# Four attention heads between the halves of two rank mixes, in an attention kernel with two mixer layers

## The chip, the cores and the metric

One core of a Trainium2 chip runs the whole program. The metric is the device time of one execution in microseconds (us), taken as the median of several runs. Three runs of the kernel before gave 1568.89, 1569.15 and 1572.46 us.

## What is computed

Four batches (448 tokens, 12 heads of 64 channels) go through three layers. The reference, cut to what matters:

```python
q_n, k_n = rmsnorm(q, g_q), rmsnorm(k, g_k)
scores = (q_n @ k_n.transpose(0, 1, 3, 2)) / sqrt(64)
x = softmax(scores) @ v                       # then heads side by side: (4, 448, 768)

u = x + ((x.transpose(0, 2, 1) @ U) @ V).transpose(0, 2, 1)      # "rank mix", rank 32
x = u + relu(u @ w_ch1) @ w_ch2                                  # 768 -> 3072 -> 768

u = x + (relu(x.transpose(0, 2, 1) @ w_tok1) @ w_tok2).transpose(0, 2, 1)   # "token mix"
out = u + relu(u @ w_ch1b) @ w_ch2b                              # 768 -> 1536 -> 768
```

## The kernel before, in words

Products are made with operands split into a high and a low part (`hi`, `lo` in fp32r), so that one product takes two or three matmuls. The engines' work is issued by a Python program whose blocks are generators. A scheduler then sets the order on each engine's queue. Each queue runs in that order.

**Attention.** `attention` is one generator over 48 heads: 24 of batches b0 and b1, then 24 of b2 and b3. One step of it (`next`) issues the softmax of one head and, in lockstep, the weighing of the head before. Softmax takes four chunks of scores: the matmuls into `sc` in PSUM, a maximum `nm` on DVE (L327), an exponential `p` on ACT (L329), a scaling of `p` on POOL (L336). Weighing takes four transposes `pt` (L355), the split into `ph` on ACT (L363) and `pl` on DVE (L367), and eight matmuls into `pv`; `tmp` (L375) and a sum on DVE (L376) end a head. For every second head a pair is loaded and normalised (POOL: `sq`, `qn`, `kn`, L255 and L273; DVE: `ms`, L256) and turned: transposes `tt` on PE (L290), `hi` and `lo` (L298 to L303), then twelve copies on the DMA queue of SP (L312, L313). Outputs of the last 24 heads go through the tile `xo` to memory.

**The first stage** takes the steps of the first 24 heads, with 3 `sc` and 4 `pt` buffers. Then pools are closed and others opened: PSUM has 2 buffers `p` (shared by `pt` and the transposes `pt_x` of a mix), 1 buffer `v` for `pv`, 2 buffers `s` (`sc` and `ps_u`), 1 buffer `t` (`tt` and `ps_h`) and 2 buffers `m` (the channel mixing).

**The rank mixes.** For each of b0 and b1, `rank_mix` runs two halves of 384 channels. A half has four token chunks `pt_x` (PE), each split on ACT (L428) and DVE (L429), eight matmuls into `ps_h`, a split of that on ACT (L451) and DVE (L452), and three times two matmuls into `ps_u`, whose result is added on DVE (L433), copied on ACT (L434) and subtracted on POOL (L435) by `split_u`.

**Channel mixing.** `ffn("a", ...)` runs 12 groups of two weight chunks. A group has 72 matmuls into `ps_g` and 72 into `ps_x`, for both batches. Each weight chunk comes as 64-bit words by DMA and is prepared on ACT (L125, L130, L144), DVE (L126, L127, L131) and POOL (L134, L145). `run(main, side, ratio)` takes attention steps of the remaining 24 heads between pieces of the channel mixing, in proportion to a weight that each piece yields:

```python
left += t * ratio
while left > 0:
    if next(side, None) is None:
        break
    left -= 1
```

With ratio 24 / 326 * 1.08 the steps are spread over the first eleven groups of the program; the scheduler takes them earlier where PE would be free.

Of the kernel before, what the change touches and what calls it, by code (L numbers as in the profile page):

```python
# [24 lines left out]
def attention_then_two_mixers(  # L25
# [49 lines left out]
    def f(x):  # L75
        return x.bitcast(F32)

    def mm(o, l, r, start, stop):
        nc.tensor.matmul(o, lhsT=l, rhs=r, start=start, stop=stop)  # L79
# [28 lines left out]
    def psum(kind, shape, name):  # L108
        pool = pools[kind]
        return pool.tile(shape, F32, tag=pool.name, name=name)  # L110
# [87 lines left out]
    def w1_chunk(nm, w, j):  # L198
        if f"{nm}1_{j}" in cache:
            return again(f"{nm}1_{j}")  # L200
        return load_w(w[:, j * P:(j + 1) * P].rearrange("(cc p) f -> p cc f", p=P), P, DM,
                      keep=f"{nm}1_{j}")
# [215 lines left out]
    def to_tokens(xT, hf):  # L418
        for c in range(NC4):
            pt = psum("p", [CP, HALF], "pt_x")  # L420
            for i in range(3):
                nc.tensor.transpose(
                    pt[:, i * P:(i + 1) * P],
                    xT[:, 3 * hf + i, c * CP:(c + 1) * CP], ident,
                )
            s = pools["new_xs"]()[:CP, :, :HALF]
            hi, lo = s[:, 0], s[:, 1]
            nc.scalar.activation(hi, pt, AF.Copy)  # L428
            nc.vector.tensor_sub(lo, pt, f(hi))  # L429
            yield hi, lo  # L430

    def split_u(xT, cc, pu, u):
        nc.vector.tensor_add(xT[:, cc], pu, xT[:, cc])  # L433
        nc.scalar.activation(u[0][:, cc], xT[:, cc], AF.Copy)  # L434
        pools["split_u"].tensor_sub(u[1][:, cc], xT[:, cc], f(u[0][:, cc]))  # L435

    def new_u():
        return [act.tile([P, CC, S], F32R, tag=t, name="u") for t in ("uh", "ul")]

    def rank_mix(xT, uv):  # L440

        u4, vh, vl = uv
        u = new_u()
        for hf in range(2):
            ph = psum("t", [P, HALF], "ps_h")
            for c, xs in enumerate(to_tokens(xT, hf)):
                for i in range(2):
                    mm(ph, u4[:, c].rearrange("p t r -> p (t r)"), xs[i],
                       c == 0 and i == 0, c == NC4 - 1 and i == 1)
            hst = pools["new_xs"]()[:, 0, :HALF]  # L450
            nc.scalar.activation(hst, ph, AF.Copy)  # L451
            nc.vector.tensor_sub(hst[2 * R:], ph[2 * R:], f(hst[2 * R:]))  # L452
            for i in range(3):
                pu = psum("s", [P, S], "ps_u")
                hs = hst[:, i * P:(i + 1) * P]
                mm(pu, hs, vh, True, False)
                mm(pu, hs, vl, False, True)
                split_u(xT, 3 * hf + i, pu, u)
        return u

    def token_mix(xT, w):

# [31 lines left out]
    def ffn(nm, w1, w2, xs, us, after, early=None, half=None, last=lambda: None,  # L494
            mid=lambda i: None):

        n = w1.shape[1] // P  # L500

        def first(u, ws):
            pg = psum("m", [P, S], "ps_g")
            wh, wl = ws
            for cc in range(CC):
                fs = slice(cc * P, (cc + 1) * P)
                mm(pg, wh[:, fs], u[0][:, cc], cc == 0, False)
                mm(pg, wl[:, fs], u[0][:, cc], False, False)
                mm(pg, wh[:, fs], u[1][:, cc], False, cc == CC - 1)
            s = pools["g"].tile([P, 2, S], F32R, tag="g", name="gs")  # L510
            gh, gl = s[:, 0], s[:, 1]
            nc.scalar.activation(gh, pg, AF.Relu)
            nc.vector.scalar_tensor_tensor(  # L513
                gl, pg, 0.0, f(gh), op0=ALU.max, op1=ALU.subtract
            )
            return gh, gl

        def second(xT, gs, ws, done=None):
            for dc in range(CC):
                px = psum("m", [P, S], "ps_x")  # L520
                ds = slice(dc * P, (dc + 1) * P)
                for i, ((gh, gl), (wh, wl)) in enumerate(zip(gs, ws)):
                    mm(px, wh[:, ds], gh, i == 0, False)
                    mm(px, wl[:, ds], gh, False, False)
                    mm(px, wh[:, ds], gl, False, i == len(gs) - 1)
                nc.vector.tensor_add(xT[:, dc], px, xT[:, dc])  # L526
                if done and dc % 3 == 2:
                    done(dc // 3)

        for j0 in range(0, n, G):  # L530
            js = range(j0, j0 + G)
            w1s = early if early and not j0 else [w1_chunk(nm, w1, j) for j in js]
            if 0 < j0 < n - G:
                gs = [[] for _ in xs]
                for ws in w1s:
                    for i, u in enumerate(us):
                        gs[i].append(first(u, ws))
                        yield 3.4
                w2s = [w2_chunk(nm, w2, j) for j in js]
                for i, xT in enumerate(xs):  # L540
                    second(xT, gs[i], w2s)
                    yield 3.4 * G
            else:
                w2s = [w2_chunk(nm, w2, j) for j in js]
                if j0:
                    last()
                for i in range(len(xs)):
                    gs = [first(us[i], ws) for ws in w1s]
                    if j0:
                        mid(i)  # L550
                    yield 3.4 * G
                    second(xs[i], gs, w2s, half and j0 and (lambda h: half(i, h)))
                    yield 3.4 * G
                    if j0:
                        after(i)
# [163 lines left out]
    def run(main, side, ratio):  # L719

        left = 0.0
        for t in main:
# [5 lines that stand above are left out]
        for _ in side:  # L728
            pass

    b0, b1, b2, b3 = range(B)
    xs = [new_x() for _ in range(2)]
    us = [None] * 2
# [5 lines left out]
    with ExitStack() as stack:  # L739
        open_pools(stack, (("hs", 1, 0), ("at", 2, 0)))  # L740
        inner = stack.enter_context(ExitStack())
        AT.update(p=12, ph=4, pl=4)
        open_pools(inner, (("pp", 1, 0), ("s", 3, 1), ("t", 1, 1), ("p", 4, 1)))
        pools["v"] = pools["p"]

        def new_xo():
            return pools["at"].tile([P, S], F32, tag="xo", bufs=1, name="xo")

        att = attention(
            [(b, hp, (), lambda xT=xT, hp=hp: xT[:, hp], lambda dst: None)  # L750
             for b, xT in zip((b0, b1), xs) for hp in range(NP)]
            + [(b, hp, (), new_xo,
                lambda dst, b=b, hp=hp: nc.sync.dma_start(xd[b][hp], dst))
               for b in (b2, b3) for hp in range(NP)], 2 * H)

        for t in att:
            if t == 8:
                pools["late"] = True
                uv = load_uv(False)
                pools["late"] = False  # L760
            if t == 2 * H - 1:
                break
        pools["late"] = True
        w1s = [w1_chunk("a", wa1, j) for j in range(G)]
        pools["late"] = False
        inner.close()
        AT.update(p=8, ph=3, pl=3)
        open_pools(stack, (("pp", 1, 0), ("g", 2 * G + 1, 0), ("p", 2, 1), ("v", 1, 1),
                           ("s", 2, 1), ("t", 1, 1), ("m", 2, 1)))
        pools["new_xs"] = lambda: pools["g"].tile([P, 2, S], F32R, tag="g", name="xs")  # L770
        for i in range(2):
            us[i] = rank_mix(xs[i], uv)


        def mix(i):
            us[i] = token_mix(xs[i], wt)

        def swap():
            for _ in att:
                pass  # L780
            stack.close()
            open_pools(rest, (("wt", 1, 0), ("x3", 1, 0), ("g", 3 * G, 0),
                              ("m", 3, 1), ("s", 2, 1), ("t", 1, 1), ("p", 2, 1)))
            open_pools(first_pair, (("xs", 6, 0), ("uv", 1, 0)))
            pools["new_xs"] = lambda: pools["xs"].tile([P, 2, HALF], F32R, tag="xs", name="xs")
            wt.extend(load_wt())
            kept.extend(load_uv(True))

        run(ffn("a", wa1, wa2, xs, us, mix, w1s, last=swap), att, 24 / 326 * 1.08)

    def fetch(pool, b):
        xT = pool.tile([P, CC, S], F32, tag="xT", name="xT")
# [61 lines left out]
```

## Time and profile before

| what | value |
|---|---|
| median of three runs | 1569.15 us |
| span of the profiled execution, first to last instruction | 1565.9 us |
| median of the runs less that span | 3.25 us |
| PE busy | 1467.3 us (94%) |
| DVE busy | 1124.4 us (72%) |
| POOL busy | 824.9 us (53%) |
| ACT busy | 731.0 us (47%) |
| mean granted clock of TensorE | 0.979 of full speed |

For the profiled execution the span is the time that is known; what lies around it is taken as the 3.25 us by which the median of the runs exceeds it. Shares are of the span. A busy PE counts from a matmul's start to its modelled end, and neighbours overlap, so the spacing of starts is the better measure of what PE can do.

### The profile page before, as it was taken

To read this page: it belongs to the slowest core of one execution; us is meant where nothing else is said; L and a number is where in the kernel's file an instruction comes from. 1 tells how busy PE (TensorE), PEld (TensorE's weight loads), DVE (VectorE), ACT (ScalarE), POOL (GpSimd) and SP (SyncE) were. 2 spreads that over 40 slices of the span, in tenths; PEclk is the share of its full clock that TensorE was granted. 3 is DMA by queue.
4 is the path that set the end of the run, shared out by engine and by line. 5 is a ranking of instruction groups with operands and counts; after the bars stand their busy time and mean duration, and the time that the engine had idled before them with its cause. 6 is when DMAs were issued, how large, how long until landed. Compare 5 with 4: busy or idle time off the path is not lost.

```text
span 1565.9 us, 21838 instructions
## 1 busy us (share of the span) xinstructions
PE 1467.3 (94%) x7522; PEld 1297.9 (83%) x7522; DVE 1124.4 (72%) x1824; ACT 731.0 (47%) x1449; POOL 824.9 (53%) x844
## 2 busy tenths in 40 slices
PE   5888877999999999999999999899999999999998
PEld 3566756888888889888888998789998999988997
DVE  6787977878888887766958776586756764576653
ACT  5786855666666665443624443342322222342311
POOL 6788886987877655554735543042443523103320
PEclk9898969999999999999999999999999999999999
DMA  6456663565654444542515540511212111101202
GB/s 168 118 143 151 153 198 99 168 190 180 196 161 147 142 146 137 183 172 69 184 39 187 187 143 23 163 58 51 71 51 69 43 51 61 66 21 51 71 21 91
DMA packets 103950, 180.97 MB, mean 116 GB/s; under 512 B 10464, under 2 KB 79552, under 8 KB 103840
## 3 DMA queue, kind: packets, MB, share of 16 engines
q1 hardware_dynamic: 103520, 179.58, 37.2%
q8 instruction: 60, 0.98, 0.3%
q14 instruction: 50, 0.41, 0.1%
q10 hardware_dynamic: 320, 0.00, 0.0%
HBM read 107.19 MB, written 36.57 MB: 92 GB/s over the span
## 4 chain that ended last, share of the span: by engine, by line
PE 65%; DVE 15%; DMA 6%; POOL 5%; ACT 4%; issue 4%; SPq 1%; DVEq 0%; POOLq 0%; ACTq 0%
PE ps_x L79 26%; PE ps_g L79 16%; PE ps_p L79 11%; PE sc L79 3%; PE pv L79 2%; PE pt L355 2%; DVE w_bits L126 2%; PE ps_u L79 2%; DVE w_bits L131 2%; PE ps_t L79 2%; DMA qr<-in_q_dram 1%; POOL w_bits L134 1%; DVE w_bits L127 1%; DVE nm L327 1%; POOL w L145 1%
## 5 line engine op out<-in xcount | busy, mean ns | idle before, releaser
L79 PE MATMUL ps_x<-gs,w 128*128 128x448 f32 x2592 | 576.4, 369 | 14.1 <-DVE xT L656 4.2
L79 PEld LDWEIGHTS ps_x<-gs,w 128*128 128x128 f32 x2592 | 484.0, 189 | 62.0 <-DVE xT L526 8.4
L79 PE MATMUL ps_g<-u,w 128*128 128x448 f32 x1584 | 343.7, 369 | 2.0 <-DVE gs L513 1.5
L79 PEld LDWEIGHTS ps_g<-u,w 128*128 128x128 f32 x1584 | 295.3, 188 | 27.8 <-DVE gs L513 1.9
L145 POOL TENSOR_TENSOR w<-w 128x768 fp32r<-128x768 f32 x44 | 85.0, 1941 | 220.0 <-ACT w L144 153.3
L134 POOL TENSOR_TENSOR w_bits<-w_bits,w_round 128x768 uint32<-128x768 uint32 (+3 forms) x80 | 142.1, 1776 | 93.8 <-DVE w_bits L131 34.0
L145 POOL TENSOR_TENSOR w<-w_bits,w 128x768 fp32r<-128x768 f32 (+3 forms) x82 | 147.8, 1809 | 79.8 <-ACT w L144 76.7
L656 DVE TENSOR_TENSOR xT<-ps_x,xT 128x448 f32<-128x448 f32 x216 | 127.9, 617 | 65.4 <-PE ps_x L79 63.6
L526 DVE TENSOR_TENSOR xT<-ps_x,xT 128x448 f32<-128x448 f32 x216 | 131.9, 616 | 39.5 <-PE ps_x L79 36.8
L336 POOL TENSOR_SCALAR p<-p,sm 112x448 f32<-112x448 f32 x192 | 135.4, 718 | 24.7 <-DVE sm L333 20.9
L329 ACT ACTIVATE p<-sc,nm 112x448 f32<-112x448 f32 x192 | 121.7, 635 | 43.6 <-DVE nm L327 37.3
L145 POOL TENSOR_TENSOR w_a<-w_a 128x384 fp32r<-128x384 f32 (+1 forms) x28 | 41.7, 1490 | 186.0 <-DVE w_t L223 142.9
L367 DVE TENSOR_TENSOR pl<-pt,ph 112x448 fp32r<-112x448 f32 x192 | 116.6, 614 | 16.9 <-ACT ph L363 16.4
L327 DVE TENSOR_REDUCE nm<-sc 112x1 f32<-112x448 f32 x192 | 116.1, 613 | 14.7 <-PE sc L79 14.2
L355 PE MATMUL pt<-ident,p 112*112 112x112 f32 x768 | 116.8, 263 | 3.8 <-POOL p L336 3.4
L363 ACT ACTIVATE ph<-pt 112x448 fp32r<-112x448 f32 x192 | 101.4, 544 | 39.9 <-PE pt L355 38.8
L126 DVE TENSOR_SCALAR w_bits<-w_bits 128x768 f32<-128x768 f32 (+3 forms) x80 | 81.9, 1023 | 47.8 <-ACT w_bits L125 47.4
L355 PEld LDWEIGHTS pt<-ident,p 112*112 112x112 f32 x768 | 92.0, 136 | 24.7 <-POOL p L336 6.7
L627 DVE TENSOR_TENSOR pu<-ps_p,pu 128x448 f32<-128x448 f32 x98 | 59.2, 619 | 70.8 <-PE ps_p L79 70.7
L130 ACT ACTIVATE w_round<-w_raw 128x768 uint32<-128x768 uint32 (+3 forms) x80 | 69.8, 872 | 73.9 <-POOL w_bits L134 71.9
L79 PE MATMUL sc<-ks,qs 128*112 128x448 f32 x192 | 81.5, 436 | 21.5 <-ACT p L329 13.3
L144 ACT ACTIVATE w<-w_bits 128x768 fp32r<-128x768 f32 (+3 forms) x82 | 65.6, 818 | 54.5 <-POOL w_bits L134 32.3
(104 smaller groups left out, 2390.6 us busy)
## 6 DMA issues: line engine op xcount, KB each, us to landing
w_raw<-in_moe_w_ch_dram SPq DMA_DIRECT2D x72, 768.0 KB, 4.4
c_a<-w_bits SPq DMA_DIRECT2D x48, 384.0 KB, 3.1
ks<-hi SPq DMA_DIRECT2D x96, 112.0 KB, 2.3
kt<-lo SPq DMA_DIRECT2D x96, 112.0 KB, 2.3
w<-c_a SPq DMA_DIRECT2D x28, 384.0 KB, 3.7
c_b<-w_bits SPq DMA_DIRECT2D x24, 384.0 KB, 3.1
w_a<-c_a SPq DMA_DIRECT2D x20, 384.0 KB, 2.9
w<-c_b SPq DMA_DIRECT2D x16, 384.0 KB, 3.5
```

Of the source, the lines that this page charges most:

```text
L79: nc.tensor.matmul(o, lhsT=l, rhs=r, start=start, stop=stop)
L126: nc.vector.tensor_scalar_max(f(w), f(w), TINY)
L134: nc.gpsimd.tensor_tensor(w, w, r, op=ALU.add)
L145: nc.gpsimd.tensor_sub(lo, w, f(hi))
L327: nc.vector.tensor_reduce(nm, sc, axis=AX.X, op=ALU.max, negate=True)
L329: nc.scalar.activation(p, sc, AF.Exp, bias=nm, accum_out=sm[:, c % 2:c % 2 + 1])
L336: nc.gpsimd.tensor_scalar(x, x, sm[:, i:i + 1], 1.0, op0=ALU.mult, op1=ALU.mult)
L355: nc.tensor.transpose(pt[:, c * CP:(c + 1) * CP], pr[c][:, kc * CP:(kc + 1) * CP], ident[:CP, :CP],)
L363: nc.scalar.activation(ph, pt, AF.Copy)
L367: nc.vector.tensor_sub(pl, pt, f(ph))
L526: nc.vector.tensor_add(xT[:, dc], px, xT[:, dc])
L656: nc.vector.tensor_add(xT[:, dc], px, xT[:, dc])
```

## The change

`rank_mix` becomes a generator, `rank_steps`, that stops after each half; the two first rank mixes run through it, and after each of their four halves one step of `attention` is issued. These are the steps of heads 24 to 27, the first four of b2. The ratio of `run` is cut from 24 to 20 parts accordingly. The other users of `rank_mix` (b2 and b3, later) are as before.

```diff
     def rank_mix(xT, uv):
+        u = new_u()
+        for _ in rank_steps(xT, uv, u):
+            pass
+        return u
+
+    def rank_steps(xT, uv, u):
 
         u4, vh, vl = uv
-        u = new_u()
         for hf in range(2):
...
                 split_u(xT, 3 * hf + i, pu, u)
-        return u
+            yield
...
         for i in range(2):
-            us[i] = rank_mix(xs[i], uv)
-
+            us[i] = new_u()
+            for _ in rank_steps(xs[i], uv, us[i]):
+                next(att)
...
-        run(ffn("a", wa1, wa2, xs, us, mix, w1s, last=swap), att, 24 / 326 * 1.08)
+        run(ffn("a", wa1, wa2, xs, us, mix, w1s, last=swap), att, 20 / 326 * 1.08)
```

The queues are the same up to the first half of the first rank mix. On PE, right after that half's transposes, the order changes so (`ps_h`, `ps_u`: rank mix; `ps_g`: channel mixing of the first group; `sc`: scores of head 24):

```order
 L79 MATMUL ps_h<-xs,w 128x384
 L422 MATMUL pt_x<-ident,xT 112x128 x3
+L79 MATMUL ps_h<-xs,w 128x384 x4
+L79 MATMUL ps_u<-w,xs 128x448 x6
+L79 MATMUL ps_g<-u,w 128x448 x3
+L79 MATMUL sc<-ks,qs 112x448
+L79 MATMUL sc<-kt,qs 112x448
+L79 MATMUL ps_g<-u,w 128x448
```

Before, the transposes of the second half followed at once. Now scores of heads 24 and 25 stand there, eight chunks in all, and the second half's transposes come behind most of the weighing of head 24.

On POOL, in the same stretch, the queue changes so (L435: the last step of `split_u`; L336: scaling of `p`; L273: `qn` and `kn` of the next pair of heads):

```order
+L336 TENSOR_SCALAR p<-p,sm 112x448 x4
+L332 TENSOR_SCALAR sm<-sm 112x2
+L336 TENSOR_SCALAR p<-p,sm 112x448 x2
+L332 TENSOR_SCALAR sm<-sm 112x2
+L336 TENSOR_SCALAR p<-p,sm 112x448 x2
+L273 TENSOR_TENSOR qn<-qr,rs 112x2x4x64
+L435 TENSOR_TENSOR u<-xT,u 128x448 x3
+L273 TENSOR_TENSOR kn<-kr,rs 112x2x4x64
```

The scaling of two heads and the normalising of a pair now stand between the two halves' L435, and `kn` stands behind the three L435 of the second half.

## Rows read from the trace of the kernel before

**Rows 1.** The page's first part: busy time and share of each engine.

```profile
PE 1467.3 (94%) x7522; PEld 1297.9 (83%) x7522; DVE 1124.4 (72%) x1824; ACT 731.0 (47%) x1449; POOL 824.9 (53%) x844
```

**Rows 2.** Windows: length, busy PE, PEld, DVE, ACT, POOL (counts), clock, DMA share, GB/s.

```profile
160.00:200.00 40.00, 35.94 (x228) 28.36 (x226) 37.39 (x80) 35.76 (x96) 35.54 (x67) 1.00 0.64 163
...
200.00:240.00 40.00, 29.25 (x111) 22.46 (x112) 29.93 (x45) 22.54 (x44) 30.35 (x33) 0.66 0.61 195
240.00:280.00 40.00, 32.09 (x154) 27.71 (x153) 29.39 (x47) 20.68 (x44) 27.85 (x29) 0.91 0.35 106
...
600.00:640.00 40.00, 39.80 (x212) 36.16 (x210) 30.99 (x50) 21.87 (x38) 19.16 (x15) 1.00 0.51 174
```

**Rows 3.** Windows by stage: rank mixes with the first group; attention; groups with attention.

```profile
213.67:297.89 84.22, 71.17 (x336) 60.18 (x337) 67.43 (x105) 47.23 (x97) 61.96 (x66) 0.84 0.44 140
...
40.00:200.00 160.00, 133.85 (x758) 101.45 (x756) 133.87 (x280) 127.04 (x332) 136.12 (x243) 0.94 0.58 143
297.89:623.78 325.89, 319.37 (x1765) 285.71 (x1764) 270.81 (x460) 210.53 (x432) 231.79 (x248) 1.00 0.53 162
255.50:297.89 42.39, 35.62 (x189) 30.96 (x188) 37.29 (x60) 22.92 (x49) 33.66 (x37) 0.96 0.54 163
```

**Rows 4.** Waits of PE from 213.67 to 297.89: total us, times, longest.

```profile
PE sc L79 <- ACT p L329: 6.2, 2, 4.6
PE ps_u L79 <- DVE xs L452: 3.7, 2, 2.4
PE ps_h L79 <- DVE xT L376: 2.0, 1, 2.0
PE ps_h L79 <- DVE xs L429: 1.5, 3, 1.0
PE ps_h L79 <- ACT xs L428: 1.0, 1, 1.0
```

**Rows 5.** Windows: granted clock (third number from the end) in three pieces.

```profile
206.00:231.00 25.00, 17.77 (x54) 13.22 (x55) 19.14 (x28) 13.82 (x27) 20.60 (x20) 0.50 0.63 212
231.00:250.00 19.00, 17.51 (x90) 14.65 (x89) 11.71 (x22) 9.95 (x21) 10.62 (x12) 0.95 0.18 63
250.00:264.00 14.00, 9.18 (x31) 7.84 (x32) 12.47 (x15) 7.17 (x15) 11.06 (x9) 0.76 0.12 26
```

**Rows 6.** Lines from 297.89 to 623.78, PE: count, busy us, mean ns, idle before.

```profile
L79 PE MATMUL ps_x<-gs,w 128*128 128x448 f32 x504 | 115.3, 369 | 3.0 <-DVE gs L513 2.6 <-DVE xT L526 0.3
L79 PE MATMUL ps_g<-u,w 128*128 128x448 f32 x504 | 109.8, 369 | 1.8 <-DVE gs L513 1.5 <-DVE xT L526 0.3
...
L79 PE MATMUL pv<-ph,vs 112*128 112x448 f32 x89 | 35.2, 396 | 0.6 <-DVE xo L376 0.6
...
L79 PE MATMUL sc<-ks,qs 128*112 128x448 f32 x82 | 33.5, 408 | 0.3 <-ACT p L329 0.2
```

**Rows 7.** Timeline of PE where the last head has ended: start, us, count.

```profile
623.78 14.81 PE L79 MATMUL ps_g<-u,w 128*128 128x448 f32 x72
638.43 1.36 PE L79 MATMUL ps_x<-gs,w 128*128 128x448 f32 x6
```

**Rows 8.** Lines from 40 to 200, DVE: the operation that ends a head.

```profile
L376 DVE TENSOR_TENSOR xT<-pv,tmp 64x448 f32<-64x448 f32 x22 | 13.4, 611 | 6.3 <-ACT tmp L375 6.0
```

**Rows 9.** Timeline of POOL: start, us, operation, idle before and its releaser.

```profile
238.99 3.38 POOL L435 TENSOR_TENSOR u<-xT,u 128x448 fp32r<-128x448 f32 x3 [2.75 <-ACT u L434]
246.38 3.44 POOL L435 TENSOR_TENSOR u<-xT,u 128x448 fp32r<-128x448 f32 x3 [4.00 <-ACT u L434]
```

**Rows 10.** Lines from 213.67 to 297.89, DVE: the weight preparation.

```profile
L131 DVE SCALAR_TENSOR_TENSOR w_bits<-w_raw,w_bits 128x768 uint32<-128x768 uint32 x7 | 11.0, 1571 | 0.0
...
L126 DVE TENSOR_SCALAR w_bits<-w_bits 128x768 f32<-128x768 f32 x7 | 8.8, 1258 | 3.2 <-ACT w_bits L125 3.2
...
L127 DVE TENSOR_SCALAR w_bits<-w_bits 128x768 uint32<-128x768 uint32 x7 | 6.3, 894 | 0.0
```

**Rows 11.** The same from 297.89 to 623.78: the line L126.

```profile
L126 DVE TENSOR_SCALAR w_bits<-w_bits 128x768 f32<-128x768 f32 x28 | 30.0, 1070 | 12.9 <-ACT w_bits L125 12.5 <-DMA kt<-lo 0.3
```

## The prediction

> **What bounds the kernel now.** I read the page's busy shares first. PE is busy 94% of the span and DVE 72% [rows 1], so over the whole program PE sets the time. Then the windows, to see where that fails. From 160 to 200 us, attention alone, DVE is busy 37.39 of 40 us; from 600 to 640 us, channel mixing with attention, PE is busy 39.80. Between them, from 200 to 280 us, no engine is full and the granted clock falls to 0.66 and 0.91 [rows 2]. That is the stage of the two rank mixes and the first group of channel mixing, and the change works there.
>
> I set that stage from 213.67 us (first `ps_h`, where the queues of the two kernels part) to 297.89 us (first `ps_g` of the second group): 84.2 us, with DVE busy 67.4, POOL 62.0, ACT 47.2 and PE 71.2 us [rows 3]. The waits of PE say what it lacks: 6.2 us for ACT's `p`, where attention starts again, 3.7 us for the split of `ps_h`, 4.5 us before `ps_h` matmuls [rows 4]. The clock stood at its lower level, 1.2 GHz, all of 206 to 231 us, and part of the time from 250 to 264 [rows 5]. So PE has room here. DVE has 16.8 us of room.
>
> **What the change moves.** Counted in the two orders up to the last `ps_x` of the first group, PE issues 28 matmuls into `sc` before and 56 now, 11 and 39 into `pv`, 28 and 84 transposes `pt`, 12 and 28 transposes `tt`: 3.5 heads more. Nothing is added over the whole program. The cut ratio keeps the heads' end near: they end in the eighth group of channel mixing before, and now almost a full group sooner. So 3.5 heads leave the stretch from 297.89 us on and enter the stage.
>
> **Saved later.** From 297.89 to 623.78 us, the end of the last head, PE is busy 319.37 of 325.89 us [rows 3]. It holds 1008 matmuls of channel mixing [rows 6]. Without attention 72 of them take 638.43 less 623.78, that is 14.65 us or 0.2035 us each [rows 7]; 1008 take 205.1 us. The other 120.8 us belong to 82 chunks of scores and 89 of weighing [rows 6], at four a head 21.4 heads on average: 5.64 us a head, or 5.34 us if PE's idle 6.5 us would stay. For 3.5 heads that is 18.7 to 19.7 us. I take 19 us, because PE is the bound there and most of its idle time is at groups' edges, not at heads.
>
> **Paid in the stage.** From 40 to 200 us 22 heads end [rows 8], so a head costs 133.87 / 22 = 6.1 us of DVE, 6.2 us of POOL and 5.8 us of ACT [rows 3]. 3.5 heads make 21.3, 21.7 and 20.2 us. The stage then holds 88.7 us of DVE, 83.7 of POOL and 67.4 of ACT. DVE is the fullest, and the stage lasts 88.7 us divided by the share of the time that DVE can be kept busy. Nothing in the trace shows rank mixes and heads together, so I bound that share:
>
> - 100%, every gap filled: 88.7 us, 4.5 longer; with 19 saved, 14.5 us faster. No stretch reaches it.
> - 93.5%, the best stretch of attention alone, 160 to 200 us [rows 2]: 94.9 us, net 8.3 faster.
> - 88.0%, from 255.5 to 297.89 us, attention with channel mixing and the same pools [rows 3]: 100.8 us, net 2.4 faster.
> - 83.7%, attention from 40 to 200 us [rows 3]: 106.0 us, net 2.8 slower.
> - 80.1%, the stage's own share now [rows 3]: 110.8 us, net 7.6 slower.
>
> A second bound, from above: if nothing overlapped, 3.5 heads at 160 / 22 = 7.27 us add 25.5 us, and the net is 6.5 us slower; it could be more, since those heads had more buffers. I take 88%, because its pools and neighbours are those of the stage now. The break-even is 103.2 us, a share of 86%.
>
> **Smaller parts.** The start of attention, now at 254 us, cost PE 6.2 us [rows 4]; it moves to right behind the first half's `ps_u`, and its wait falls where PE has little else. I count no gain beyond the share above. On SP, the twelve copies of each turned pair and the loads of q, k and v move ahead of the weight loads of the second group. The scheduler keeps as many preparations (seven, counted on DVE) in front of the stage's end, so I cost that at nothing. Their cover is the 72 `ps_x` of the first group; if it went, `ps_g` of the second group would wait for its chunk; the longest single wait of PE in the later groups, 2.6 us [rows 6], is the price of such a miss. On PE the clock may stay low longer while DVE sets the pace; then PE is not the bound, and its cost lies in the chosen share.
>
> **The added wait.** POOL now has `kn` of the next pair behind the three L435 of the second half. L435 waits for ACT, which waits for the end of that half; before, such waits left POOL idle 2.75 and 4.00 us, with nothing urgent behind [rows 9]. Now `kn`, the `tt` transposes on PE, and through the one buffer `t` also `ps_h` of the second batch stand behind them. What is late next is the second rank mix and with it the first `ps_x`.
>
> **Sum.** 1565.9 + 16.6 - 19 = 1563.5 us of span. The profiled execution stands 3.25 us below the median of the runs, so 1566.8 us against 1569.15. 0.3%, about what a measurement of this kernel can tell from no change, is 4.7 us: this is inside it.
>
> **Rivals.**
>
> *The gaps fill (faster).* The rank mix is a chain from PE to ACT to DVE and back, and leaves each idle in turn [rows 4, 9]; heads are independent of it and can fill all of that. DVE would run at 93.5%, the stage takes 94.9 us, and the time is 1560.9 us. It decides from 98.5 us down, a share over 90%. For it: 16.8 us of DVE idle time now, and PE much less loaded than in the later groups. Against it: only 2 buffers for scores and 2 for `pt` and `pt_x` together. The Trainium skill, in Perfetto Trace Analysis, section Optimization Strategy, says that regimes with different contended engines may gain when they are interleaved; no run here shows it for these two.
>
> *They take turns (slower).* The mechanism is the added wait: POOL's queue and the buffers `t`, `p` and `s`, which heads and rank mix share, make one stand still while the other runs. Then the stage keeps its 80.1%, takes 110.8 us, and the time is 1565.9 + 26.6 - 19 + 3.25 = 1576.7 us. It decides from 107.9 us up, a share under 82.2%. For it: PE's order has the second half's transposes behind the weighing of a head, and `tt` in front of `ps_h`. Against it: it needs almost as much time as no overlap at all.
>
> *DVE's weight work stretches.* One L126 lasts 1.258 us in the stage on average, L131 1.571 and L127 0.894, together 26.1 us [rows 10]. If they grow with POOL's share, from 62.0 / 84.2 = 74% to 83.7 / 103 = 81%, that adds 2.6 us of DVE, 3.0 us of stage, and gives 1569.8 us. Against it: with POOL 71% busy in the later groups [rows 3] L126 takes 1.070 us [rows 11], so POOL's share alone doesn't set it. The Trainium skill, in GPSIMD Engine Reference, section Specifications, states that POOL shares its SBUF interfaces with DVE and that both contend in certain DVE instructions; by that rule this case holds, by the row on the later groups the sum above does.
>
> *The scheduler undoes it.* Excluded: the orders show the heads moved.
>
> **How the numbers follow.** The forecast case gets 0.32 and the stretched weight work 0.08, both within 0.3%; all gaps filled 0.37, since any share over 90% is enough and the room is there; taking turns 0.23. That gives faster 0.37, same 0.40, slower 0.23. The range goes from 1558.0 us (3 us beyond the faster case, a share of 97%) to 1577.0 us (the slower case). The forecast's own range is 1564.4 to 1573.9 us, the 0.3% on both sides.
>
> **What would show it.** The first `ps_g` of the second group should start near 314.5 us (213.67 + 100.8) instead of 297.89, with DVE at about 88% from 213.67 to there, and the last head should end some 19 us earlier, relative to that point, than the 325.9 us of now. If the stage ends before 312 us, the faster case holds; past 321.5 us with PE waiting at `ps_h` and `tt`, the slower one. The sum is wrong in its saved part if PE's idle time from there to the last head is far from 6.5 us, and in its stage part if DVE's busy time there is far from 88.7 us.

## The result, and the profile after

The changed kernel took 1581.91 us (median of six runs, 1576.82 to 1590.36), the kernel before 1569.02 us in the same comparison: a ratio of 1.0095, 95% interval 1.0069 to 1.0121. In a second comparison (e13 below) it was 1579.08 against 1568.78 us, ratio 1.0059, 1.0031 to 1.0086. One of the eight executions behind the 1579.08 us ran at a granted clock of 0.565 and took 2355.70 us; the ratio leaves it out. So the change makes the kernel slower by 10 to 13 us, by the medians. The forecast was 1566.8 us and its range ended at 1577.0.

The first profile of the changed kernel is the slowest of its six runs (1590.36 us, span 1588.6). Its stage is therefore shown beside that of a second profile of each kernel (that of the kernel before is the slowest of eight runs, 1576.77 us). Lines from L440 on stand five higher in the changed kernel (L452 is L457, L526 is L531). Columns as in [rows 3]: length, busy us of PE, PEld, DVE, ACT and POOL, granted clock, DMA share, GB/s. The first row is the stage, the second goes from there to the end of group eight. The changed kernel, first profile:

```profile
214.39:328.77 114.38, 94.86 (x456) 75.35 (x456) 88.23 (x148) 68.60 (x152) 80.44 (x101) 0.88 0.44 130
328.77:642.00 313.23, 304.60 (x1644) 272.74 (x1644) 246.80 (x418) 189.68 (x376) 206.25 (x214) 0.99 0.52 164
```

The changed kernel, second profile:

```profile
211.73:325.35 113.62, 93.34 (x457) 73.90 (x457) 88.29 (x148) 68.85 (x152) 80.31 (x101) 0.90 0.45 133
325.35:634.80 309.45, 301.58 (x1644) 270.51 (x1645) 246.97 (x418) 189.67 (x376) 207.07 (x214) 1.00 0.53 166
```

The kernel before, second profile (its first is in [rows 3], with 326.11 us from 297.89 to 624.00):

```profile
213.91:297.52 83.61, 70.47 (x336) 59.18 (x337) 67.24 (x105) 47.33 (x97) 62.00 (x66) 0.86 0.46 145
297.52:625.40 327.88, 320.49 (x1766) 287.21 (x1765) 271.04 (x460) 210.64 (x432) 230.75 (x248) 0.99 0.52 161
```

The stage takes 114.4 and 113.6 us instead of 84.2 and 83.6: 30.1 us more on average. DVE has 88.2 us of work in it, as forecast, but is busy for 77% of it only. The fullest engine is PE, before and after: it is busy 94.1 us on average instead of 70.8, and idle 19.9 us instead of 13.1. So of the 30.1 us, 23.3 are added busy time of PE and 6.8 added idle time. Behind the stage 311.3 us on average stand against 327.0: 15.7 us saved, with 12.9 and 18.4 us in the two pairs of profiles. The balance, +14.4 us, is the slowdown, within the spread of these runs.

Where the 30 us lie is seen on PE's timeline, in the `ps_u` matmuls that end each half of a rank mix (columns: start, us, operation, count, idle before). The kernel before, first `ps_u` of each of the four halves, then the last:

```profile
223.69 1.86 PE L79 MATMUL ps_u<-w,xs 128*128 128x448 f32 x4 [2.43 <-DVE xs L452]
...
236.77 1.07 PE L79 MATMUL ps_u<-w,xs 128*128 128x448 f32 x4
...
244.47 0.97 PE L79 MATMUL ps_u<-w,xs 128*128 128x448 f32 x4
...
250.20 1.86 PE L79 MATMUL ps_u<-w,xs 128*128 128x448 f32 x4 [1.24 <-DVE xs L452]
253.01 0.82 PE L79 MATMUL ps_u<-w,xs 128*128 128x448 f32 x2
```

The same in the changed kernel, with what PE waited for in between:

```profile
223.57 1.86 PE L79 MATMUL ps_u<-w,xs 128*128 128x448 f32 x4 [3.71 <-DVE xs L457]
...
251.39 1.00 PE L79 MATMUL ps_u<-w,xs 128*128 128x448 f32 x4
...
265.06 0.31 PE L355 MATMUL pt<-ident,p 112*112 112x112 f32 x1 [1.10 <-POOL p L336]
...
267.19 0.62 PE L355 MATMUL pt<-ident,p 112*112 112x112 f32 x2 [0.83 <-POOL p L336]
267.49 1.84 PE L79 MATMUL ps_u<-w,xs 128*128 128x448 f32 x4
...
282.72 1.06 PE L79 MATMUL ps_u<-w,xs 128*128 128x448 f32 x4
...
284.42 0.57 PE L79 MATMUL ps_u<-w,xs 128*128 128x448 f32 x2
```

The halves, 13, 8 and 6 us apart before, are now 28, 16 and 15 us apart. The last `ps_u` begins 31.4 us later, and from there to the second group the stage is as long as before: 44.9 us (253.01 to 297.89) and 44.4 us (284.42 to 328.77). So 3.5 heads lengthen the mixes by 8.6 us each (30.1 / 3.5), more than a head takes alone (7.27 us). Nothing of them was hidden in the mixes' gaps: PE's idle time grew. The same lines show what the clock costs: four `ps_u` take 1.84 to 1.86 us where the granted clock is 0.50 (1.2 GHz) and 0.97 to 1.07 us where it is 1.00 (2.4 GHz).

DVE's lines show where it stood still. L327, the maximum over a chunk of scores (columns: busy, mean ns, idle before and its releaser), in the changed kernel:

```profile
L327 DVE TENSOR_REDUCE nm<-sc 112x1 f32<-112x448 f32 x28 | 17.2, 617 | 10.1 <-PE sc L79 9.8
```

Of DVE's 26.1 us of idle time (114.38 less 88.23) 10.1 us come right before it, waiting for PE's scores. In the kernel before the largest wait of DVE there was for `xs` (5.9 us), and 0.7 us stood before L327. On POOL one wait stands out, for the pair that is loaded next (timeline of POOL, changed kernel):

```profile
252.87 1.04 POOL L273 TENSOR_TENSOR qn<-qr,rs 112x512 f32<-112x512 f32 x1 [8.41 <-PE tt L290]
253.87 3.38 POOL L435 TENSOR_TENSOR u<-xT,u 128x448 fp32r<-128x448 f32 x3
257.22 1.03 POOL L273 TENSOR_TENSOR kn<-kr,rs 112x512 f32<-112x512 f32 x1
```

`kn` does stand behind the three L435, as forecast; but `qn` ahead of them has already waited 8.41 us for PE to read the buffer that it overwrites.

### The profile page after: what moved, and what is told of

It is laid out like the page before. It is cut to its first block, busy times and chain, and to the rows that moved or that the text cites. A ratio compares the mean times of both kernels' runs of the same rounds, so it can differ in the third digit from the quotient of the medians.

```text
span 1588.6 us, 21842 instructions
## 1 busy us (share of the span) xinstructions
PE 1481.2 (93%) x7522; PEld 1305.5 (82%) x7522; DVE 1123.0 (71%) x1824; ACT 731.6 (46%) x1449; POOL 818.4 (52%) x844
## 4 chain that ended last, share of the span: by engine, by line
PE 63%; DVE 14%; POOL 6%; DMA 6%; ACT 5%; issue 5%; SPq 1%; ACTq 0%; POOLq 0%; DVEq 0%
PE ps_x L79 26%; PE ps_g L79 14%; PE ps_p L79 10%; PE sc L79 3%; PE pt L355 2%; PE pv L79 2%; DVE w_bits L126 2%; PE ps_u L79 2%; PE ps_t L79 2%; DVE w_bits L131 1%; POOL w_bits L134 1%; DMA qr<-in_q_dram 1%; ACT p L329 1%; POOL w L145 1%; ACT w_bits L125 1%
## 5 line engine op out<-in xcount | busy, mean ns | idle before, releaser
L79 PE MATMUL ps_x<-gs,w 128*128 128x448 f32 x2592 | 580.0, 371 | 18.1 <-DVE xT L531 6.1
L531 DVE TENSOR_TENSOR xT<-ps_x,xT 128x448 f32<-128x448 f32 x216 | 132.8, 617 | 50.5 <-PE ps_x L79 46.8
L336 POOL TENSOR_SCALAR p<-p,sm 112x448 f32<-112x448 f32 x192 | 128.4, 682 | 18.2 <-DVE sm L333 16.6
L327 DVE TENSOR_REDUCE nm<-sc 112x1 f32<-112x448 f32 x192 | 115.7, 614 | 22.3 <-PE sc L79 21.7
L355 PEld LDWEIGHTS pt<-ident,p 112*112 112x112 f32 x768 | 93.2, 138 | 26.1 <-POOL p L336 8.3
L126 DVE TENSOR_SCALAR w_bits<-w_bits 128x768 f32<-128x768 f32 (+3 forms) x80 | 77.9, 973 | 49.3 <-ACT w_bits L125 49.0
```

What stands on the lines that cost most here:

```text
L126: nc.vector.tensor_scalar_max(f(w), f(w), TINY)
L327: nc.vector.tensor_reduce(nm, sc, axis=AX.X, op=ALU.max, negate=True)
L336: nc.gpsimd.tensor_scalar(x, x, sm[:, i:i + 1], 1.0, op0=ALU.mult, op1=ALU.mult)
L355: nc.tensor.transpose(pt[:, c * CP:(c + 1) * CP], pr[c][:, kc * CP:(kc + 1) * CP], ident[:CP, :CP],)
```

## The experiments

Three theories. **A:** heads and rank mix hinder each other, in POOL's queue (**A1**) or through the PSUM buffers that they take in turn (**A2**: `s` for `sc` and `ps_u`, `t` for `tt` and `ps_h`). **B:** heads in the stage cost by their amount of work, wherever they stand. **C:** the cost is the thinner spread of heads over channel mixing. Each kernel was compared in five rounds (e14 in one).

**e1: the ratio alone.** The kernel before with

```diff
-        run(ffn("a", wa1, wa2, xs, us, mix, w1s, last=swap), att, 24 / 326 * 1.08)
+        run(ffn("a", wa1, wa2, xs, us, mix, w1s, last=swap), att, 20 / 326 * 1.08)
```

> The kernel before with only the ratio cut from 24 to 20: rank mixes untouched, no head moved in front of the channel mixing. Theory A (heads and rank mix hinder each other in POOL's queue and in shared buffers): within 4 us of before, the stage from the first ps_h to the first ps_g of the second group stays at 84 us within 3. Theory B (four heads packed into one place cost more there than they save later, whatever stands around them): the same. Theory C (the loss lies in the thinner spread of heads over the later groups, not in the stage): slower than before by 5 us or more, with the stage at 84 us.

Measured: 1570.60 us, ratio 1.0023 (1.0006 to 1.0039). The stage is as before:

```profile
210.22:294.21 83.99, 70.67 (x336) 59.34 (x337) 66.15 (x105) 47.69 (x98) 62.19 (x67) 0.86 0.46 142
```

C can make up 0.2%, not 0.6 to 1.0%.

**e2 and e3: four heads behind both mixes, or ahead of both.** With the ratio of e1 and

```diff
+        for _ in range(4):
+            next(att)
```

behind (e2) or ahead of (e3) the loop of the two rank mixes.

> The same four heads, ratio 20, issued behind both rank mixes and ahead of the first group, not between the halves. Theory A: rank mixes run as before, heads no longer stand between their halves, so less is lost: 0 to 7 us slower than before, and no wait of POOL for a transpose of more than 5 us in the stage. Theory B: as slow as the change, 10 to 16 us, since as many heads are packed into the stage. Theory C: 5 us or more slower, with the later stretch as in the change.

> The same four heads, ratio 20, issued ahead of both rank mixes. Theory A: 0 to 7 us slower than before, as with the heads behind them. Theory B: 10 to 16 us slower. If this one is much worse than the heads behind the rank mixes, the start of the channel mixing, which needs the rank mixes, is what the heads hold up.

Measured: e2 1567.18 us, ratio 1.0005 (0.9991 to 1.0020). PE's order up to the last `ps_x` of group one then holds the 28 score matmuls of before, so the scheduler put the heads back to where they stood, and the run shows that the early issue alone costs nothing; against B it says little. e3 1578.79 us, ratio 1.0087 (1.0072 to 1.0103). Its group one ends 36 us later with some 4.6 heads more by then (counted from its `sc`, `pv` and `pt`), 7.8 us a head, near the 7.27 us of attention alone; groups two to eight take 27.1 us less, 5.9 us a head:

```profile
333.76:633.70 299.94, 295.10 (x1596) 264.25 (x1595) 238.62 (x402) 180.47 (x355) 199.11 (x199) 1.00 0.52 166
```

So a head ahead of channel mixing pays back less than it costs alone; only one that is hidden in the mix can gain.

**e4: one head in each mix, not two.** The changed kernel with a head behind the first half only, and 22 in place of 20:

```diff
-            for _ in rank_steps(xs[i], uv, us[i]):
-                next(att)
+            for hf, _ in enumerate(rank_steps(xs[i], uv, us[i])):
+                if hf == 0:
+                    next(att)
```

> Two heads instead of four, one behind the first half of each rank mix, ratio 22. Theory A: the load of the next pair and its place in POOL's queue come with the second head, so the loss is half of the change's or less, 0 to 6 us. Theory B: half of the loss, 5 to 8 us. If it is as slow as the change, what costs is the place where a half is cut, not the number of heads.

Measured: 1582.23 us, ratio 1.0097 (1.0079 to 1.0114), as slow as four heads.

```profile
214.16:324.62 110.46, 87.77 (x424) 70.99 (x425) 85.57 (x138) 63.84 (x140) 77.36 (x95) 0.88 0.43 127
```

2.5 heads (by PE's order) cost 26.6 us, DVE at 77.5%. Half of the slowdown or less was expected from A, so the number of heads alone is not what counts. What both have in common is a head inside a mix.

**e5: L435 off POOL (A1).** In the two first mixes the subtractions of `split_u` go to DVE:

```diff
+        pools["split_u"] = nc.vector
         for i in range(2):
...
+        pools["split_u"] = nc.gpsimd
```

> The changed kernel with one edit: in the first pair's two rank mixes the subtractions that split u (the L435 of POOL, 12 of them, 1.1 us each in the trace of the changed kernel) go to DVE. The scheduler then also orders PE's rows a little otherwise. Theory A1 (POOL's queue: the loads of the next pairs of heads, qn and kn, stand behind three L435 and come late, 8.4 us of POOL waiting at L273): POOL's queue is 13 us shorter in the stage and DVE has some 7 us more on it; the stage falls from 114.4 to about 105 us and the time to about 1573 us, 9 us under the changed kernel. Theory A2 (the banks of PSUM that the mix and the heads share in one order, t for ps_h, tt and pt_x, s for sc and ps_u): the chain of waits is the same, with DVE longer on it; stage 114 to 121 us, time 1582 to 1589 us. Theory B (the amount of work on DVE in the stage): DVE 88 to 95 us, time about 1589 us.

Measured: 1580.27 us, ratio 1.0086 (1.0054 to 1.0118). Window of the stage, and POOL's wait:

```profile
215.01:338.26 123.25, 101.87 (x485) 81.08 (x485) 100.19 (x172) 74.55 (x165) 75.49 (x99) 0.86 0.45 131
```
```profile
POOL qn L273 <- PE tt L290: 10.4, 2, 10.2
```

PE's order also took in 0.5 head more, and DVE has 12 us more work; the stage is longer than any theory had it. A1 alone falls: with no L435 of these mixes in POOL's queue `qn` waits for PE as long as before, and the stage does not shorten.

**e6: `ps_h` out of the buffer `t` (A2, first half).** The changed kernel with `ps_h` of the first pair in the buffers `m`:

```diff
-            ph = psum("t", [P, HALF], "ps_h")
+            ph = psum("t" if late else "m", [P, HALF], "ps_h")
```

> The changed kernel with one edit: ps_h of the first pair's two rank mixes is taken from the PSUM buffers m (two) in place of t (one), so that tt and pt_x need not wait for ps_h to be read. Theory A2: the wait of tt of the next pair behind ps_h goes, qn and kn are not held (8.4 us of POOL's wait at L273), and the stage falls by 5 to 10 us: time 1572 to 1577 us. Theory A1: tt is earlier, but the loads still stand behind three L435 of POOL; the stage falls by 0 to 4 us, time 1578 to 1582 us. Theory B: no change, 1580 to 1583 us.

Measured: 1580.60 us, ratio 1.0075 (1.0051 to 1.0099), within the two results of the changed kernel. The stage and the longest wait of POOL in it:

```profile
209.25:333.13 123.88, 103.62 (x483) 81.48 (x484) 94.00 (x160) 74.69 (x165) 89.04 (x112) 0.83 0.45 134
```
```profile
POOL u L435 <- ACT u L434: 11.5, 2, 11.1
```

The wait of `qn` is gone, and one of 11.5 us for the rank mix's `u` stands in its place, with 4.2 heads moved by PE's order. POOL's queue holds whichever of the two comes late, so neither wait alone is the cause. A kernel with the edits of e5 and e6 together was not run.

**e7: `ps_u` out of the buffers `s`, no head moved.** The kernel before with

```diff
-                pu = psum("s", [P, S], "ps_u")
+                pu = psum(kind, [P, S], "ps_u")
...
-            us[i] = rank_mix(xs[i], uv)
+            us[i] = rank_mix(xs[i], uv, "m")
```

> The kernel before with one edit: ps_u of the first pair's two rank mixes is taken from the PSUM buffers m in place of s, which it shared with sc of the heads. By its order PE then has the score matmuls of the first heads of the stage already between the matmuls of the two rank mixes, though nobody moved a head in the program. Theory A2 (it is the shared ring s, handed out in the order of the program, that keeps heads out of the gaps of the rank mix): heads start earlier in the stage for nothing; the stage falls from 84.2 to some 78 to 81 us and the time by 3 to 6 us, to about 1561 to 1564 us. Theory A1 (POOL's queue) and B (amount of work, DVE 67 us busy either way): no gain, 1565 to 1568 us; A1 allows a loss of up to 4 us if the heads' sq and p delay L435.

Measured: 1572.48 us, ratio 1.0016 (0.9996 to 1.0037).

```profile
213.06:305.05 91.99, 79.01 (x414) 65.73 (x415) 75.66 (x133) 60.73 (x135) 73.77 (x87) 0.95 0.49 150
305.05:629.70 324.65, 310.26 (x1687) 275.94 (x1686) 259.37 (x433) 195.61 (x394) 215.79 (x228) 1.00 0.53 162
```

The stage did not shorten, and the time is 3.5 us above the kernel before in the same comparison, within the loss of up to 4 us that A1 allowed. But the 2.4 heads that the scheduler now put between the mixes cost only 8.1 us, 3.4 a head. That they overlap is not shown: PE is idle 13.0 us, as in the kernel before (13.1), and the granted clock is 0.95 against 0.84 and 0.86. By the two levels that is some 10 us at 1.2 GHz instead of 27 and 23; if PE sets the pace, half of the difference, 6 to 9 us (an estimate), is the clock's. The expected gain failed since the time behind the stage fell by 2.3 us only, with PE idle for 14.4 us there.

**e8: two heads behind each whole mix.** The changed kernel with

```diff
-            us[i] = new_u()
-            for _ in rank_steps(xs[i], uv, us[i]):
-                next(att)
+            us[i] = rank_mix(xs[i], uv)
+            next(att)
+            next(att)
```

> The changed kernel with one edit: the four heads are issued two and two behind each whole rank mix, and no longer inside one. Half of them (two) still stand ahead of the second rank mix. Theory A (a head inside a mix cuts it in two and each half waits for the head's buffers and POOL work): the cut is gone, two heads ahead of the second mix cost about 7.3 less 5.3 us each, 4 us: time 1569 to 1573 us. Theory B (heads ahead of the channel mixing cost by their number, 3.5 moved): time 1578 to 1583 us, as the changed kernel. Theory C (the share of heads among channel mixing alone): as the kernel with the ratio alone, 1568 to 1571 us.

Measured: 1574.38 us, ratio 1.0036 (1.0015 to 1.0057).

```profile
211.64:317.03 105.39, 88.94 (x440) 71.45 (x441) 85.43 (x140) 65.52 (x143) 79.83 (x95) 0.89 0.48 142
317.03:630.50 313.47, 305.29 (x1661) 272.48 (x1660) 249.48 (x425) 192.35 (x386) 213.95 (x220) 1.00 0.53 164
```

Between A's numbers and B's, nearer A's. A mix that is not cut costs less: 2.9 heads for 21.5 us (7.4 a head), DVE at 81.1%. DVE's work is that of e4 (85.6 us), so amount alone (B) does not explain the difference of 5.1 us in their stages; nor does the clock, 0.89 against 0.88. PE is idle 16.4 us here and 22.7 us in e4.

**e9 and e10: `ps_u` out of `s` with the heads moved.** The changed kernel (e9) and e8's kernel (e10) with the two mixes' `ps_u` in `m`, as in e7.

> The changed kernel with one edit: ps_u of the first pair's two rank mixes is taken from the PSUM buffers m in place of s, the two that it shares with sc of the heads in the order of the program. PE's order then has 5.5 heads more in the stage than the kernel before (sc 72 against 28), where the changed kernel has 3.5 more. Theory A2 (the shared buffers s make heads and mix take turns, and that is why a moved head cost 9.0 us of the stage in the changed kernel, and 3.2 us in the kernel before with this same edit): 5.5 heads cost about 18 to 25 us of the stage, group one ends at 316 to 323 us instead of 329, and later 5.5 heads save 3.9 to 5.3 us each, 21 to 29 us: time 1560 to 1573 us. Theory D (what a head costs is its own chain over DVE, POOL and ACT, some 7 us whatever the buffers): 5.5 heads cost 38 us or more, group one ends past 333 us, time 1577 to 1586 us.

> The changed kernel with two edits: two heads behind each whole rank mix, none inside one, and ps_u of both mixes in the PSUM buffers m. PE's order then has 4.5 heads more in the stage than the kernel before. The one with the first edit alone paid 7.0 us of the stage for each of 2.9 heads and came out at 1574.4 us. Theory A2: with s free for sc the price falls to 3 to 5 us a head, 14 to 22 us for 4.5, saved later 4.8 us each, 22 us: group one ends at 312 to 320 us, time 1561 to 1570 us. Theory D: 7 us each, 32 us, group one ends near 329 us, time 1577 to 1580 us.

Measured: e9 1583.79 us, ratio 1.0091 (1.0068 to 1.0113); e10 1567.67 us, ratio 1.0009 (0.9989 to 1.0028). Stage and what follows of e9:

```profile
212.57:333.33 120.76, 106.68 (x530) 85.84 (x530) 100.11 (x173) 77.80 (x179) 93.92 (x119) 0.89 0.49 142
333.33:638.60 305.27, 296.02 (x1571) 263.82 (x1571) 240.31 (x393) 178.12 (x349) 192.41 (x196) 0.99 0.51 161
```

and of e10:

```profile
211.82:316.84 105.02, 92.70 (x500) 77.03 (x501) 89.01 (x162) 74.43 (x170) 87.94 (x112) 0.94 0.53 155
316.84:625.50 308.66, 298.84 (x1602) 266.35 (x1601) 241.11 (x403) 182.07 (x359) 203.06 (x202) 0.99 0.52 162
```

e10 has 0.8 us more of DVE work in the stage than the changed kernel, 1.1 heads more (4.6), and a stage 9.0 us shorter, DVE at 84.8%. So as much work of DVE in the same stage is 9 us cheaper when no mix is cut and `sc` and `ps_u` no longer share buffers. PE's idle time makes up 7 to 8 us of that: 12.3 us instead of 19.5 and 20.3. Its busy time is 92.7 us instead of 94.9 and 93.3, though it does a head more. There the clock may have helped: 0.94 against 0.88 and 0.90, by the two levels some 13 us at 1.2 GHz instead of 27 and 23; if PE sets the pace, that is worth 5 to 7 us (an estimate), much of the added head. So the 9 us are not shown to be the buffers and the cut alone. e9, cut but with `s` free, came out near D's numbers: 5.6 heads cost 36.9 us. A head costs 6.6 us there against 8.6, and PE's idle time is 14.1 us, nearly that of the kernel before, at a clock of 0.89. e10, not cut, came out at A2's numbers and not at D's. DVE's wait for scores, L327, in e8, e9 and e10:

```profile
L327 DVE TENSOR_REDUCE nm<-sc 112x1 f32<-112x448 f32 x25 | 15.4, 614 | 4.0 <-PE sc L79 4.0
```
```profile
L327 DVE TENSOR_REDUCE nm<-sc 112x1 f32<-112x448 f32 x35 | 21.3, 615 | 2.9 <-PE sc L79 2.6
```
```profile
L327 DVE TENSOR_REDUCE nm<-sc 112x1 f32<-112x448 f32 x32 | 19.5, 613 | 1.7 <-PE sc L79 1.6
```

It falls from 10.1 us to 4.0 without the cut, to 2.9 with `s` free, and to 1.7 with both. It is no measure of the price, though: in e5, with the cut and the shared `s`, it fell to 4.3 us while the stage grew.

```profile
L327 DVE TENSOR_REDUCE nm<-sc 112x1 f32<-112x448 f32 x31 | 18.9, 612 | 4.3 <-PE sc L79 4.1
```

**e11 and e12: a thinner spread for the two best.** e7 with 22 for 24, e10 with 18 for 20 heads per 326 steps.

> The kernel before with two edits: ps_u of the first pair's rank mixes in the PSUM buffers m, and 22 in place of 24 heads per 326 steps of channel mixing. With the first edit alone the stage took 7.4 us more for 2.3 heads, but the groups two to eight saved 1.7 us only, with PE idle 14 us in them against 6.5 before, and the heads ran out at 616.8 us, 13 us ahead of that group's end. Theory R (the heads left were issued too densely for channel mixing): with the thinner ratio they reach to the end of group eight, PE's idle time there goes back to 7 us, time 1564 to 1567 us, 5 to 8 us under the one edit alone. Theory D' (saved time of groups two to eight is lost for another reason, as at the hand-over from the stage): no change, 1570 to 1574 us.

> The changed kernel with two heads behind each whole rank mix, ps_u of both mixes in the PSUM buffers m, and 18 in place of 20 heads per 326 steps of channel mixing. With 20 it came out at 1567.7 us; its heads ran out at 591.2 us, 34 us ahead of the end of group eight, and PE was idle some 10 us in groups two to eight against 6.5 in the kernel before. Theory R (the heads that are left stand too densely): PE's idle time there goes to 6 or 7 us, time 1563 to 1566 us, a little faster than the kernel before. Theory S (a thinner spread gives nothing back, as with 22 for 24): 1567 to 1571 us.

Measured: e11 1571.51 us, ratio 1.0023 (1.0004 to 1.0042); e12 1568.78 us, ratio 1.0004 (0.9984 to 1.0024). Their stages repeat those of e7 and e10 (90.4 and 104.9 us). The ratio is no lever, and no kernel tried here beats the kernel before.

**e13 and e14: both kernels once more,** nothing edited, for a second profile of each.

> The changed kernel once more, nothing edited, for a second profile. Theory M (the stage's length comes from the order of the work): the stage from the first ps_h to the second group's first ps_g takes 112 to 117 us again with DVE at 76 to 79%, and groups two to eight end some 13 us sooner counted from there; time 1578 to 1586 us. Theory Z (the profile was an outlier in the stage itself): the stage takes 102 to 108 us with DVE above 82%.

> The kernel before once more, nothing edited, for a second profile. Theory M: stage 83 to 86 us with DVE at 79 to 81%, and 326 us from there to the last head. Theory Z: the stage differs from 84.2 us by 4 us or more, or the stretch behind it from 326 us by as much.

Measured: e13 1579.08 us, ratio 1.0059 (1.0031 to 1.0086); e14 1569.42 us, ratio 0.9998 (0.9977 to 1.0019). The windows are those at the top: the stages repeat to 0.8 us, so M holds for them. Behind the stage one execution of the changed kernel differs from the next by 3.8 us, which is the spread that a reading of that part has.

Together (heads by PE's order up to the last `ps_x` of group one; "cost" is the stage less 83.9 us, "PE busy" and "PE idle" are by how much PE's busy time in the stage, as the profile counts it, exceeds 70.8 us and its idle time 13.1 us; "saved" is 327.0 us less the stretch to the end of group eight; all four references are the means of the two profiles of before):

| kernel | mix cut | `s` shared | heads | cost, us | PE busy, us | PE idle, us | a head | DVE share | clock | saved, us | ratio |
|---|---|---|---|---|---|---|---|---|---|---|---|
| changed | yes | yes | 3.5 | 30.1 | +23.3 | +6.8 | 8.6 | 77.4% | 0.88, 0.90 | 15.7 | 1.0095, 1.0059 |
| e4 | yes | yes | 2.5 | 26.6 | +17.0 | +9.6 | 10.6 | 77.5% | 0.88 | 13.2 | 1.0097 |
| e5 (L435 on DVE) | yes | yes | 4.0 | 39.4 | +31.1 | +8.3 | 9.8 | 81.3% | 0.86 | 25.7 | 1.0086 |
| e6 (`ps_h` in `m`) | yes | yes | 4.2 | 40.0 | +32.8 | +7.2 | 9.5 | 75.9% | 0.83 | 27.3 | 1.0075 |
| e9 | yes | no | 5.6 | 36.9 | +35.9 | +1.0 | 6.6 | 82.9% | 0.89 | 21.7 | 1.0091 |
| e8 | no | yes | 2.9 | 21.5 | +18.1 | +3.4 | 7.4 | 81.1% | 0.89 | 13.5 | 1.0036 |
| e10 | no | no | 4.6 | 21.1 | +21.9 | -0.8 | 4.6 | 84.8% | 0.94 | 18.3 | 1.0009 |
| e7 | no | no | 2.4 | 8.1 | +8.2 | -0.1 | 3.4 | 82.2% | 0.95 | 2.3 | 1.0016 |

Cost less saved gives each ratio within 4 us, but for the changed kernel's second one (5 us). The expectations of e9 and e10 reckoned 9.0, 3.2 and 7.0 us a head for the changed kernel, e7 and e8; the table has 8.6, 3.4 and 7.4. PE's added idle time sorts the kernels: 7 to 10 us with a cut mix and `s` shared, 3.4 us without the cut, 1 us or less with `s` free. That is what heads and mixes cost each other. The larger part of each cost is PE's own busy time for the heads. A price a head mixes both with the clock and with the number of heads that the scheduler moved, so the price of a single cut is not isolated.

## Why the prediction was wrong

**The step that failed** is the share of the stage that DVE can be kept busy: "I take 88%, because its pools and neighbours are those of the stage now". It was 77.1% and 77.7%, below every share of the list, the stage's own 80.1% included. The stage term, 16.6 us in the sum, measured 30.1 us, more than the serial bound of 25.5, of which the prediction had said that it could be more. Three things were wrong in it.

First, PE was left out of the sum ("So PE has room here"), although [rows 3] has it busy for 71.2 us of the stage, longer than DVE. By the same rows a head costs 133.85 / 22 = 6.1 us of PE, so the stage would hold 92.5 us of PE against 88.7 of DVE, and PE was busy for 84.0% of the very stretch from which DVE's 88% was taken. 92.5 / 0.84 makes 110.1 us of stage and a time of 1576 us. PE was busy for 94.9 and 93.3 us, 83% and 82% of the stage.

Second, the 88% itself holds a stall. The stretch begins in the middle of one L126 of 4.92 us, a line that takes 1.07 us on average later [rows 11], and 3.8 of the 37.3 us of busy DVE are that one instruction (timeline of DVE, kernel before):

```profile
254.41 4.92 DVE L126 TENSOR_SCALAR w_bits<-w_bits 128x768 f32<-128x768 f32 x1
```

Without it DVE is busy for 79%. The second profile of before has the same with 4.80 us. What stretched it was not tested.

Third, the stretch has no rank mix in it. Its heads fill in between channel mixing, which shares the engines with them but has PSUM buffers of its own, `m`. In the changed stage mix and head share the buffers `s`, `t` and `p`, and the order on PE puts one's matmuls behind the other's results. The experiments show this part as PE's added idle time, 6.8 us: it is 3.4 us with no mix cut, 1.0 us with `s` free, and gone with both. The break-even share that the prediction worked out, 86%, was reached by none, and no kernel was faster.

**What was right.** The amount of work: 3.5 heads moved; DVE 88.2 us in the stage against 88.7 forecast, ACT 68.6 against 67.4, POOL 80.4 against 83.7. Which engine is fullest among DVE, ACT and POOL, though PE is fuller than all three. The serial price of a head, 7.27 us: heads ahead of both mixes (e3) paid 7.8.

**Saved later** was 19 us in the sum and is 15.7 us, 12.9 and 18.4 in the two pairs. Part of the lower figure is the single execution: the `ps_x` matmuls of the same groups are slower in the first profile of the changed kernel, where the granted clock was 0.50 from 624.8 to 631.6 us, than in the second, where it was 1.00 throughout (lines of PE behind the stage: busy, mean ns, idle before), first and second profile:

```profile
L79 PE MATMUL ps_x<-gs,w 128*128 128x448 f32 x504 | 118.8, 377 | 5.5 <-DVE gs L518 4.5 <-DVE xT L531 1.0
```
```profile
L79 PE MATMUL ps_x<-gs,w 128*128 128x448 f32 x504 | 115.9, 370 | 4.9 <-DVE gs L518 3.9 <-DVE xT L531 1.0
```

With both terms as measured, the prediction's sum is 1565.9 + 30.1 - 15.7 + 3.25 = 1583.6 us; of the 16.8 us that it lies above the forecast, 13.5 are the stage's and 3.3 the saved part's.

**Smaller parts.** The wait at the start of attention did not fall away: PE waits 5.2 us for `p` ahead of `sc` in the stage against 6.2 [rows 4], and 2.6 us more for POOL's `p` (waits of PE, changed kernel):

```profile
PE sc L79 <- ACT p L329: 5.2, 4, 2.7
PE ps_u L79 <- DVE xs L457: 3.7, 1, 3.7
PE pt L355 <- POOL p L336: 2.6, 4, 1.1
PE ps_h L79 <- DVE xT L376: 2.0, 1, 2.0
```

The clock does not explain the difference of these two kernels: 0.88 and 0.90 over the longer stage against 0.84 and 0.86, by the two levels some 27 and 23 us at 1.2 GHz in each.

**The rivals.** "They take turns" came true with a larger price than its 80.1%: it gave 1576.7 us. Its marker, a second group past 321.5 us, held (328.77 and 325.35). Its mechanism was half right: the shared buffers count, but POOL's L435 alone does not (e5), and PE waited at `sc` and `pt` more than at `ps_h` and `tt`. It deserved more than 0.23, since PE's order, with the next half's transposes behind the weighing of a head, was open to see. "The gaps fill" failed because a head between two halves is not independent of them as far as buffers and queues go; its 94.9 us would also have needed PE, with 92.5 us of work, busy for 97.5%. The Trainium skill, in Perfetto Trace Analysis, section Optimization Strategy, says that a kernel whose most-contended engine changes over time may gain when its regimes are interleaved. The runs here show no gain in time, neither with the mixes cut (1.0095 and 1.0059) nor with whole mixes and `s` free (e10, 1.0009). "The weight work stretches" fell: 24.5 us in the stage against 26.1 [rows 10], although POOL was busy for 80.4 us beside it instead of 62.0 (lines of DVE, changed kernel):

```profile
L131 DVE SCALAR_TENSOR_TENSOR w_bits<-w_raw,w_bits 128x768 uint32<-128x768 uint32 x7 | 9.8, 1406 | 0.0
L126 DVE TENSOR_SCALAR w_bits<-w_bits 128x768 f32<-128x768 f32 x7 | 9.7, 1384 | 1.3 <-ACT w_bits L125 1.3
...
L127 DVE TENSOR_SCALAR w_bits<-w_bits 128x768 uint32<-128x768 uint32 x7 | 5.0, 721 | 0.0
```

**What stays open.** Whether a cut costs through PE's order (the next half's `pt_x` behind a head's `pv`) or through the buffers `p` that `pt` and `pt_x` share was not separated. Nor was the part of the clock in the low prices of e7 and e10, nor why it was granted higher there. Nor is it known why e7 and e11, whose heads cost least in the stage, saved only 2.3 and 5.4 us behind it.

## What to carry to other kernels

Add up the moved work on every engine of the stage, the one that bounds the rest of the program first: here PE was the fullest in both places, so moving heads could gain, apart from the clock, at most the 13.1 us that PE was idle. Idle time in a stage is room for other work only if that work does not share the stage's buffers and does not stand between two links of its chain on an in-order queue; look up which buffers both take and in which order before a share of busy time is borrowed from a stretch where they don't meet, and look in that stretch for a single stretched instruction that counts as busy. Moved work costs its serial time until a trace shows the overlap, and it must cost less there than it gives back where it came from: here 8.6 us a head against 4.5. Where the balance is a difference of two terms of 20 to 30 us, a few points of the assumed share decide its sign, and the chances should say so.

## What was not expected of the hardware

One wait was traded for another of much the same size: with `ps_h` in the buffers `m` (e6) POOL's 8.4 us ahead of `qn` went, and 11.5 us ahead of L435 came. And two profiles of one program lie 11.9 us of span apart (1588.6 and 1576.7 us), more than the effect of most edits here, while the stage in them differs by 0.8 us: 2.7 us come ahead of it, 3.8 us in the groups behind it, and 4.9 us after group eleven. Their mean granted clocks are 0.974 and 0.980, by the two levels some 20 us more at 1.2 GHz in the longer one; if PE sets the pace that is worth 10 us, an estimate that covers most of the difference.
